# Four attention tiles in float32 instead of nine: where the exponentials and values become float16 pairs

## The chip, the cores and the metric

One core of one Trainium2 chip runs the whole program in one launch. The metric is the device time of one execution in microseconds. The kernel before took 1939.94 us (median of three runs, 1937.46 to 1942.82).

## The reference

Three stages follow one another on 4 sequences of 576 tokens with 8 heads of 64, so 2304 tokens of 512 features:

```
scores = q @ k.T / sqrt(64) - slope[head] * |i - j|     # only for 0 <= i - j < 128
attn   = exp(scores - max) / (sum + 1e-9);  x = attn @ v
x = relu(x @ w_in)**2 @ w_out                            # 512 -> 2048 -> 512
P = exp(x @ w_gate - max), then 8 times: rows / sum, columns / sum, times N/E
out = sum over 8 experts e of P[:, e] * (relu(x @ w1[e]) @ w2[e])   # 512 -> 1024 -> 512
```

q, k and v are float32; w_in and w_out come as float64 words and are narrowed to float32 in the kernel.

## The kernel before

**Pairs.** Most products are computed on float16 pairs: a number is scaled by a power of two and split into a high float16 part (a ScalarE copy) and a low one (the rest, by VectorE or by GpSimd in `minus`, L407). A product of two pairs is three matmuls (high x high, high x low, low x high).

**Attention tiles.** 18 tiles of 128 queries: tiles 0 to 3 and 4 to 7 are the full tiles of sequences 0 and 1, tile 8 holds the 64 last queries of both; 9 to 17 are the same for sequences 2 and 3. A tile needs its own keys and those of the tile before it (`prevs`): tile 0, 4, 9 and 13 have no tile before them, tile 8 needs tiles 3 and 7. Per tile SyncE loads q, k and v into the ring `raw` (8 slots), TensorE turns q and k in float32 (`turn`), and then four steps j of two heads each follow: `scores` (float32 matmuls into one bank), `bias` (VectorE adds the distance and takes the maximum, into a buffer `e`, of which there are 3), `expo` (ScalarE).

From there tiles differ. With `PAIRED = 9` tiles 0 to 8 stay in float32: TensorE turns the exponentials (`turn_e`, L632), ScalarE copies them out of the bank (`turned_e`, L637), and TensorE gathers them with the raw values (`gather`, L654). v's slot of `raw` is held until the next tile has gathered. Tiles 9 to 17 are paired: ScalarE and GpSimd split the exponentials (`e_hi` L520, `e_lo`), SyncE turns both halves by a DMA transpose (`flip_e`, L410), and TensorE gathers pairs (`gather_pairs`, L550). Their values are scaled by a norm (`v_norm` on ScalarE, `v_sum` on TensorE, `v_scale` as small VectorE operations) and split (`v_hi` L499, `v_lo` L502); `join_v` (L515) brings the earlier tile's values to the same scale. The paired values lie in a room of four slots with the tag `yacc`, which is also the tag of block 0's accumulator, so `v_hi` waits for block 0's end (`ready_y[0]`).

Then both kinds divide by the sum, are split and turned by another transpose into xT (`settle`, `x_hi`, `x_lo`, `flip_x`).

**First feed-forward stage.** Blocks hold 4, 2, 4, 4 and 4 tiles, in parts m of 256 tokens (part 0 has 512). For each of 16 slices f of the hidden width: `h_part` (L1032, 12 matmuls of 256 columns), `h_relu` (ScalarE, from the bank to `r`), `h_square` (VectorE, in `r`), `h_hi` and `h_lo`, `y_part` (L1069, 12 matmuls). h has two banks, r two and sq four buffers. Part 0 goes through the four chunks g of w_in and w_out as they come: each chunk is read through SyncE into `stage`, narrowed by VectorE (`narrow`, L887 to L895), scaled and split. The second stage (experts, from about 550 us to the end) is not touched.

**Order.** All of it is planned while the program is built: each step is a unit with an engine, a cost, a rank, the units it waits for and the slots it takes. `Plan.run` plays these costs through and fixes every engine's order; ready units go by rank, and the attention tiles' ranks (100 a tile) stand before those of the feed-forward matmuls. DMAs are all issued by SyncE, in the order of the plan; a waiting one holds up those behind it. Until a planned 66 us `keep_warm` fills TensorE with idle matmuls (L291). The slots of `raw`, `e`, `eT`, `vo` and some more are handed out in the order in which the units were made.

Of the kernel before, what the change touches and what calls it, by code (L numbers as in the profile page):

```python
# [15 lines left out]
HI, LO = 0, 1  # L16
# [131 lines left out]
def kernel(  # L148
# [74 lines left out]
    unit_s = const.tile([P, 2, NCH], F32, name="unit_s")  # L223
# [90 lines left out]
    def make_tail():  # L314
# [10 lines left out]
            raw=8, qT=2, kT=5, s=1, sp=1, diag=1, e=3, eh=2, eT=3, vo=4, vp=1, av=1, x=1, xh=1, x0=1, x1=1, xb=1, yacc=1,  # L325
# [50 lines left out]
    EXPS, TURNED = 3, 3  # L376
# [88 lines left out]
    PAIRED = 9  # L465
    assert not any(x < PAIRED for i in range(PAIRED, NTILE) for x in prevs(i))

# [10 lines left out]
    def v_scale(i):  # L478

        m = main[i]  # L480
        sc = scale_v[i] = small.tile([P, 2], F32, tag="sc", bufs=8, name=f"sc{i}")
        yield from pow2_of_norm((sc[:, 0:1],), m.pop("vss"), 1, WHOLE)
        for x in m["pv"]:
# [5 lines left out]
        for x in m["pv"]:  # L489
            yield  # L490
            f = tiny(1, "fs", bufs=6)
            DVE.tensor_tensor(out=f, in0=scale_v[x][:, 0:1], in1=sc[:, 1:2], op=ALU.mult)
            m["fs"].append(f)

    def v_hi(i):
        if "room" not in values:
            values["room"] = ap_.tile([P, 4, 2, H, D], F16, tag="yacc", name="values")
        values[i] = values["room"][:, plan.got["vo"]]
        ACT.activation(out=values[i][:, HI], in_=raw[i, 2], func=ACTF.Copy, scale=scale_v[i][:, 1:2])  # L499

    def v_lo(i):
        DVE.scalar_tensor_tensor(  # L502
            out=values[i][:, LO], in0=raw.pop((i, 2)), scalar=scale_v[i][:, 1:2], in1=values[i][:, HI], op0=ALU.mult,
            op1=ALU.subtract,
        )
# [156 lines left out]
    def plan_tile(i):  # L662
# [19 lines left out]
        a["kT"], a["v"] = T[1], ld[2]  # L682
        jv = None
        if paired(i):
            n = len(pv)
            u = unit(ACT, c_act(W), v_norm, i, rank=z, after=[ld[2], st])
            mx = unit(PE, 0.3, v_sum, i, rank=z, take=["s"], after=[constants["ones"], u])
            us = chain(DVE, [TINY] * (3 + 2 * n), v_scale, i, rank=z, after=[mx, *(done[p]["sc"] for p in pv)])
# [6 lines left out]
            if pv:  # L695
                older = [] if full else [x for p in pv for x in done[p]["uses"]]
                jv = unit(
                    DVE, 0.43 * n, join_v, i, rank=z + 6, take=["vp"] if full else [],
                    after=[*(done[p]["v"] for p in pv), a["sc"], *older],
                )  # L700
# [29 lines left out]
        for p in (*pv, i):  # L730
            plan.free(done[p]["kT"][0], "kT", *S)
            if not paired(i):
                plan.free(done[p]["v"], "raw", *G)
# [124 lines left out]
    def w_out_scale(g):  # L858

        yield from pow2_of_norm((out_s[:, 0, g : g + 1], out_s[:, 1, g : g + 1]), wst.pop(("out", g)), 1, WHOLE)  # L860
        yield
        DVE.scalar_tensor_tensor(
            out=unit_s[:, 0, g : g + 1], in0=in_s[:, 0, g : g + 1], scalar=in_s[:, 0, g : g + 1],
            in1=out_s[:, 0, g : g + 1], op0=ALU.mult, op1=ALU.mult,
        )
        if g == NCH - 1:
            yield
            m = tiny(2, "cm")
            DVE.tensor_reduce(out=m[:, 0:1], in_=unit_s[:, 0, :], op=ALU.max, axis=AX.X)
# [4 lines left out]
            yield  # L874
            DVE.tensor_scalar(out=gain, in0=m[:, 0:1], scalar1=2.0**14, scalar2=None, op0=ALU.mult)
# [54 lines left out]
    def plan_weights(kind, g, z):  # L930
# [32 lines left out]
        if kind == "out":  # L963
            sq = [unit(ACT, c_act(n), w_sumsq, g, x, rank=z, after=[nr[x], *early]) for x in parts]
            plan.order(sq[1], sq[0])
            ad = unit(DVE, TINY, w_out_add, g, rank=z, after=sq)
            al = unit(PE, 0.3, w_sum, kind, g, rank=z, take=["s"], after=[ad, constants["ones"]])
            us = chain(
                DVE, [TINY] * (8 if g == NCH - 1 else 4), w_out_scale, g, rank=z,
                after=[al, wready["in", g][0], *wready.get(("out", g - 1), [])[:1]],  # L970
            )
            plan.free(al, "s", us[0])
            sc = us[-1]
# [63 lines left out]
    def h_relu(m, f, c):  # L1037
        if f % 2 == 0:
            hold["r", c] = big.tile([P, 2, MC], F32, tag="r", bufs=2, name=f"r{m}_{f}_{c}")
        r = hold["r", f, c] = hold["r", c][:, f % 2]  # L1040
        ACT.activation(out=r, in_=hold.pop(("h", f, c)), func=ACTF.Relu, scale=2.0**-7)  # L1041

    def h_square(m, f, c):
        r = hold["r", f, c]
        g = f // FPC
        if m:
            DVE.scalar_tensor_tensor(out=r, in0=r, scalar=unit_s[:, 1, g : g + 1], in1=r, op0=ALU.mult, op1=ALU.mult)  # L1047
        else:
            DVE.tensor_tensor(out=r, in0=r, in1=r, op=ALU.mult)

    def h_hi(m, f, c):
        if f % 2 == 0:
            hold["sq", c] = big.tile([P, 2, 2, MC], F16, tag="sq", bufs=4, name=f"sq{m}_{f}_{c}")
        sq = hold["sq", f, c] = hold["sq", c][:, f % 2]
        ACT.activation(out=sq[:, HI], in_=hold["r", f, c], func=ACTF.Copy)  # L1055

    def h_lo(m, f, c):
        sq = hold["sq", f, c]
        minus(sq[:, LO], hold.pop(("r", f, c)), sq[:, HI])

    def y_part(m, f, d, c):

        sq = hold["sq", f, c] if d < KD - 1 else hold.pop(("sq", f, c))
        w = pair_of("out", f // FPC)
        first, last = (f % FPC == 0, f % FPC == FPC - 1) if m == 0 else (f == 0, f == KF - 1)
        if first and d % 2 == 0:
            hold["y", d // 2] = pa_.tile([P, 2, MC], F32, tag="ya", bufs=2, name=f"y{m}_{f}_{c}_{d}")
        for a, b in PAIRS:
            PE.matmul(  # L1069
                hold["y", d // 2][:, d % 2], lhsT=w[:, a, f % FPC, d * P : (d + 1) * P], rhs=sq[:, b],  # L1070
# [4 lines left out]
    def y_add(g, c, b):  # L1075
# [3 lines left out]
        y, t, s = hold["yacc"][:, 2 * b : 2 * b + 2, c : c + MC], hold.pop(("y", b)), unit_s[:, 0, g : g + 1]  # L1079
# [8 lines left out]
    def y_src(m, b):  # L1088
        return hold["yacc"][:, b : b + 1] if m == 0 else hold["y", b]
# [6 lines left out]
    def y_max(m, b):  # L1096
        n = y_srcs(m)
        if b == 0:
            hold["ym"] = tiny(n, f"ym{n}")
        DVE.tensor_reduce(  # L1100
            out=hold["ym"][:, b : b + 1], in_=y_src(m, b), op=ALU.max, axis=AX.XY, apply_absolute_value=True
        )
        if b == n - 1:
            t = tiny(1, "ymx")
            DVE.tensor_reduce(out=t, in_=hold["ym"], op=ALU.max, axis=AX.X)
            hold["ym"] = t

# [21 lines left out]
    def y_hi(m, b):  # L1129
# [16 lines left out]
    def plan_block(m):  # L1146
# [10 lines left out]
        for f, c in steps:  # L1157
# [3 lines left out]
            deps = [*xs[(c - c0) // P : (c - c0 + MC) // P], *wready["in", g]]  # L1161
            h0 = unit(PE, c_pe(6, MC), h_part, m, f, c, 0, rank=z - 100 * LEAD, take=["h"], after=deps)
# [207 lines left out]
    free_forms += [lambda: big.tile([P, 2, KH, 2 * P], F16, tag="sq", bufs=4, name="form")] * 4  # L1370
    free_forms += [lambda: big.tile([P, 2, KH, 2 * P], F16, tag="r", bufs=2, name="form")] * 2
# [529 lines left out]
    with tc.manual_schedule():  # L1901
# [11 lines left out]
        for i in range(PAIRED):  # L1913
# [53 lines left out]
```

## Time and profile before

| | us |
|---|---|
| median of three runs | 1939.94 |
| the profiled execution | 1941.23 |
| its span | 1939.5 |
| TensorE busy | 1893.8 (98%) |
| VectorE busy | 1605.7 (83%) |
| ScalarE busy | 1256.2 (65%) |
| GpSimd busy | 938.6 (48%) |

The span runs from the first instruction to the last. Busy time is the union of an engine's instructions. PE is TensorE, PEld its weight loads, DVE VectorE, ACT ScalarE, POOL GpSimd, SP SyncE (SPq: what its queue issues).

### The profile page before, as it was taken

What the parts mean: (1) busy time and instruction counts of PE and PEld (TensorE: products, weight loads), DVE (VectorE), ACT (ScalarE), POOL (GpSimd) and SP (SyncE); (2) the same over time, 40 slices, a digit from 0 to 9 for tenths busy, and PEclk for the clock granted to TensorE, in tenths of its full rate; (3) what the DMA queues carried; (4) which work ended last, traced back from release to release, by engine and by line L of the source; (5) the groups of instructions that cost most, each with busy time, mean ns of one, the idle gap of its engine ahead of it and who ended that gap; (6) DMA issues with size and microseconds to landing.
All of it is one profiled execution on the core that took longest, in us unless ns stands there. A gap on an engine that the chain in (4) does not pass through costs nothing.

```text
span 1939.5 us, 47163 instructions
## 1 busy us (share of the span) xinstructions
PE 1893.8 (98%) x18458; PEld 1680.8 (87%) x18458; DVE 1605.7 (83%) x3897; ACT 1256.2 (65%) x3434; POOL 938.6 (48%) x1198
## 2 busy tenths in 40 slices
PE   9999999999998999999999999999999999999999
PEld 9788888888876888898888989888898888888898
DVE  6796675455549898899989899899989989999887
ACT  5777576354345787666767676676766667666663
POOL 3445354356635654545535445454544545445432
PEclk9999999999999999999999999999999999999999
DMA  9455264210010010110101011000101101010002
GB/s 244 122 145 108 60 117 77 43 52 1 2 45 12 23 34 23 34 33 13 34 23 34 12 34 34 23 23 23 34 13 34 34 23 34 13 34 13 2 23 77
DMA packets 159663, 85.36 MB, mean 44 GB/s; under 512 B 112080, under 2 KB 144848, under 8 KB 159440
## 3 DMA queue, kind: packets, MB, share of 16 engines
q1 hardware_dynamic: 159440, 82.35, 16.6%
q8 instruction: 144, 2.36, 0.5%
q14 instruction: 79, 0.65, 0.1%
HBM read 64.50 MB, written 4.72 MB: 36 GB/s over the span
## 4 chain that ended last, share of the span: by engine, by line
PE 82%; DVE 11%; ACT 3%; DMA 2%; issue 1%; POOL 0%; SPq 0%; DVEq 0%; POOLq 0%; ACTq 0%
PE oX L1520 17%; PE X L1438 16%; PE h L1032 9%; PE oY L1520 8%; PE y L1069 8%; PE Y L1438 8%; PE Z L1438 4%; PE oZ L1520 4%; DVE hp L1501 4%; PE s L593 2%; DVE late L1340 1%; DMA stage<-in_moe_w_dram 1%; PE av L654 1%; PE warm L291 1%; PE t L569 1%
## 5 line engine op out<-in xcount | busy, mean ns | idle before, releaser
L1438 PEld LDWEIGHTS <-late 128*128 128x128 f16 x6720 | 617.8, 98 | 95.1 <-issue 29.6
L1520 PEld LDWEIGHTS <-hp 128*128 128x128 f16 x6048 | 584.0, 98 | 69.4 <-DVE hp L1501 3.3
L1520 PE MATMUL oX<-late,hp 128*128 128x256 f16 x3456 | 468.3, 273 | 2.9 <-DVE hp L1501 2.3
L1501 DVE TENSOR_TENSOR hp<-late,hp 128x256 f16<-128x256 f32 (+1 forms) x669 | 337.4, 524 | 10.1 <-ACT hp L1497 8.1
L1497 ACT ACTIVATE hp<-late 128x256 f16<-128x256 f32 (+1 forms) x669 | 248.0, 387 | 21.3 <-POOL late L1487 7.7
L1501 DVE TENSOR_TENSOR hp<-x,hp 128x256 f16<-128x256 f32 (+1 forms) x451 | 242.9, 549 | 14.7 <-ACT hp L1497 13.3
L1438 PE MATMUL Y<-y,late 128*128 128x256 f16 (+1 forms) x1920 | 241.4, 262 | 1.3 <-ACT late L1466 1.2
L1520 PE MATMUL oY<-late,hp 128*128 128x256 f16 x1728 | 233.5, 273 | 0.0
L1478 ACT ACTIVATE late<-late 128x256 f32<-128x256 f32 (+1 forms) x286 | 111.2, 393 | 165.9 <-DVE late L1470 164.7
L1069 PE MATMUL y<-sq,w_out 128*128 128x256 f16 x1728 | 215.7, 273 | 2.2 <-DVE yacc L1083 1.2
L1438 PE MATMUL X<-late 128*128 128x256 f16 (+1 forms) x1728 | 204.9, 255 | 12.8 <-DVE late L1470 7.4
L1032 PE MATMUL h<-xT,w_in 128*128 128x256 f16 x1728 | 216.4, 274 | 0.0
L407 POOL TENSOR_TENSOR sq<-r,sq 128x256 f16<-128x256 f32 x144 | 106.7, 742 | 211.4 <-ACT sq L1055 204.3
L1069 PEld LDWEIGHTS <-w_out 128*128 128x128 f16 x1728 | 166.4, 98 | 23.5 <-issue 1.7
L1032 PEld LDWEIGHTS <-w_in 128*128 128x128 f16 x1728 | 167.7, 98 | 21.2 <-issue 0.5
L407 POOL TENSOR_TENSOR stage<-stage 128x256 f32<-128x256 f32 x210 | 168.5, 803 | 34.4 <-ACT hp L1497 21.9
L1497 ACT ACTIVATE hp<-x 128x256 f16<-128x256 f32 (+1 forms) x451 | 172.2, 388 | 15.8 <-POOL x L1487 6.2
L1438 PE MATMUL X<-form,late 128*128 128x256 f16 x1152 | 157.1, 272 | 3.7 <-DVE x L1470 2.1
L1340 DVE SCALAR_TENSOR_TENSOR late<-stage,es,late 128x512 f16<-128x512 f32 (+2 forms) x180 | 158.5, 909 | 0.7 <-ACT late L1336 0.6
L1047 DVE SCALAR_TENSOR_TENSOR r<-r,unit_s 128x256 f32<-128x256 f32 x112 | 68.7, 616 | 100.7 <-ACT r L1041 99.9
L1478 ACT ACTIVATE x<-x 128x256 f32<-128x256 f32 (+1 forms) x194 | 74.5, 389 | 118.0 <-DVE x L1470 117.3
L1487 POOL TENSOR_TENSOR late<-late 128x256 f32<-128x256 f32 (+1 forms) x58 | 45.7, 787 | 196.1 <-DVE hp L1501 170.1
(230 smaller groups left out, 3230.9 us busy)
## 6 DMA issues: line engine op xcount, KB each, us to landing
stage<-in_moe_w_dram SPq DMA_DIRECT2D x60, 256.0 KB, 3.2
stage<-in_moe_w_dram SPq DMA_DIRECT2D x30, 512.0 KB, 3.7
st_in<-in_moe_w_in_dram SPq DMA_DIRECT2D x16, 512.0 KB, 6.6
st_out<-in_moe_w_out_dram SPq DMA_DIRECT2D x16, 512.0 KB, 4.8
raw_q<-in_q_dram SPq DMA_DIRECT2D x16, 256.0 KB, 4.4
raw_k<-in_k_dram SPq DMA_DIRECT2D x16, 256.0 KB, 4.3
raw_v<-in_v_dram SPq DMA_DIRECT2D x16, 256.0 KB, 4.5
out_dram<-acc_wc SPq DMA_DIRECT2D x8, 256.0 KB, 2.3
```

Source lines behind the costliest of these rows:

```text
L407: POOL.tensor_tensor(out=dst, in0=src, in1=hi, op=ALU.subtract)
L593: PE.matmul(sp[:, n, P : 2 * P], lhsT=q_, rhs=keys[i][r, j], start=True, stop=True)
L1032: PE.matmul(hp, lhsT=w[:, a, kk, r], rhs=xT[parts1[m][0]][:, b, kk, c : c + MC], start=(kk == 0 and a == b), stop=(kk == KD - 1 and a == LO),)
L1047: DVE.scalar_tensor_tensor(out=r, in0=r, scalar=unit_s[:, 1, g : g + 1], in1=r, op0=ALU.mult, op1=ALU.mult)
L1069: PE.matmul(hold["y", d // 2][:, d % 2], lhsT=w[:, a, f % FPC, d * P : (d + 1) * P], rhs=sq[:, b], start=(first and d % 2 == 0 and a == b) ...
L1340: DVE.scalar_tensor_tensor(out=lo, in0=t, scalar=es[:, g, 2 * kind + 1 : 2 * kind + 2], in1=hi, op0=ALU.mult, op1=ALU.subtract)
L1438: PE.matmul(pt, lhsT=w[:, a, row(kk), :], rhs=rhs, start=(x in (1, 2, 5) and kk == 0 and a == c), stop=(x in (2, 3, 4) and kk == KH - 1 an ...
L1478: ACT.activation(out=t, in_=src, func=ACTF.Relu)
L1487: POOL.tensor_tensor(out=c, in0=c, in1=b, op=ALU.add)
L1497: ACT.activation(out=f[:, HI], in_=hold["t", PLACE[name], g, j, p], func=ACTF.Copy)
L1501: DVE.tensor_tensor(out=f[:, LO], in0=hold["t", PLACE[name], g, j, p], in1=f[:, HI], op=ALU.subtract)
L1520: PE.matmul(pt[:, t], lhsT=f[:, a, t * P : (t + 1) * P], rhs=w[:, c, row], start=(x in (1, 2, 5) and p == t == 0 and a == c), stop=(x in ( ...
```

## The change

`PAIRED` goes from 9 to 4: tiles 4 to 8 are paired too. Tile 3 stays in float32, but since tile 8 needs its values, they are scaled and split as well. The values get a room of five slots of their own, so `v_hi` no longer waits for block 0; `raw` has 6 slots for 8 and `e` 2 for 3. All tiles are planned ahead of all blocks, in one loop each. Small sums on TensorE (`v_sum`, `w_sum` of w_out) wait themselves for what the VectorE chain behind them needed. From part 2 on `h_square` multiplies h, still in its bank, by relu(h) in `r`, with the factor 2^-7 in a third column of `unit_s`; the bank is freed by the square, and h waits for w_out's last scale. The names kept in `hold` carry the part, and r and sq take fixed slots.

```diff
-    unit_s = const.tile([P, 2, NCH], F32, name="unit_s")
+    unit_s = const.tile([P, 3, NCH], F32, name="unit_s")
-            raw=8, ..., e=3, eh=2, eT=3, vo=4, ...
+            raw=6, ..., e=2, eh=2, eT=3, vo=5, ...
-    EXPS, TURNED = 3, 3
+    EXPS, TURNED = 2, 3
-    PAIRED = 9
+    PAIRED, VALUES = 4, 5
 def v_scale(i):
+        pv = m["pv"] if paired(i) else []
 def v_hi(i):
-            values["room"] = ap_.tile([P, 4, 2, H, D], F16, tag="yacc", name="values")
+            values["room"] = ap_.tile([P, VALUES, 2, H, D], F16, tag="values", name="values")
 def plan_tile(i):
-        if paired(i):
-            n = len(pv)
+        if paired(i) or any(i in prevs(x) for x in range(PAIRED, NTILE)):
+            n = len(pv) if paired(i) else 0
-            mx = unit(PE, 0.3, v_sum, i, rank=z, take=["s"], after=[constants["ones"], u])
-            us = chain(DVE, ..., v_scale, i, rank=z, after=[mx, *(done[p]["sc"] for p in pv)])
+            mx = unit(PE, 0.3, v_sum, ..., after=[constants["ones"], u, *(done[p]["sc"] for p in pv if n)])
+            us = chain(DVE, ..., v_scale, i, rank=z, after=[mx])
-            vh = unit(ACT, c_act(W), v_hi, i, rank=z + 9, take=["vo"], after=[a["sc"], *ready_y[0]])
+            vh = unit(ACT, c_act(W), v_hi, i, rank=z + 9, take=["vo"], after=[a["sc"]])
-            a["v"] = unit(DVE, c_dve(W, 1.17), v_lo, i, rank=z + 11, after=[vh])
-            plan.free(ld[2], "raw", a["v"])
+            a["vl"] = unit(DVE, c_dve(W, 1.17), v_lo, i, rank=z + 11, after=[vh])
+            plan.free(ld[2], "raw", a["vl"])
+            if paired(i):
+                a["v"] = a["vl"]
 def w_out_scale(g):
+            DVE.tensor_scalar(out=unit_s[:, 2, :], in0=unit_s[:, 1, :], scalar1=2.0**-7, ...)
 def plan_weights(kind, g, z):
-            al = unit(PE, 0.3, w_sum, kind, g, rank=z, take=["s"], after=[ad, constants["ones"]])
+            al = unit(PE, 0.3, w_sum, ..., after=[ad, constants["ones"], wready["in", g][0], ...])
 def h_square(m, f, c):
-            DVE.scalar_tensor_tensor(out=r, in0=r, scalar=unit_s[:, 1, g : g + 1], in1=r, ...)
+            s = unit_s[:, 1 + (m > 1), g : g + 1]
+            DVE.scalar_tensor_tensor(out=r, in0=h if m > 1 else r, scalar=s, in1=r, ...)
 def plan_block(m):
+            if m > 1:
+                deps.append(wready["out", NCH - 1][0])
-            plan.free(h0, "h", r)
+            q_.shared = m < 2
+            plan.free(h0, "h", q_ if m > 1 else r)
 ...
-        for i in range(PAIRED):
+        for i in range(NTILE):
             plan_tile(i)
-        plan_block(0)
-        for i in range(PAIRED, NTILE):
-            plan_tile(i)
-        for m in range(1, NM):
+        for m in range(NM):
             plan_block(m)
```

## Rows read from the trace of the kernel before

**Rows 1.** Busy time of each engine by stretch; bracketed are instruction counts.

```profile
core 0: us, PE busy (x) PEld busy (x) DVE busy (x) ACT busy (x) POOL busy (x), PEclk, DMA share, GB/s
66.00:84.00 18.00, 15.05 (x133) 13.40 (x134) 13.78 (x47) 14.33 (x37) 7.39 (x5) 1.00 0.15 31
84.00:140.00 56.00, 53.56 (x479) 46.49 (x479) 47.59 (x112) 42.23 (x96) 30.29 (x29) 0.97 0.60 161
140.00:183.00 43.00, 43.00 (x395) 36.27 (x396) 30.16 (x87) 32.64 (x80) 19.21 (x19) 1.00 0.34 88
183.00:236.00 53.00, 53.00 (x495) 45.85 (x493) 30.82 (x103) 32.59 (x94) 19.99 (x26) 1.00 0.40 72
236.00:400.00 164.00, 161.44 (x1786) 137.47 (x1783) 101.32 (x308) 96.84 (x281) 70.67 (x81) 1.00 0.45 81
400.00:550.00 150.00, 148.21 (x1412) 131.80 (x1410) 73.54 (x132) 62.78 (x146) 90.55 (x106) 1.00 0.04 14
```

**Rows 2.** The filler tile: ns min/median/max, then first and last start, forms.

```profile
L291 PE MATMUL warm<-ones x460: 219/219/314, 1.1 to 65.8; 128*128 128x128 f16 x154
```

**Rows 3.** The gathers' tile, as above.

```profile
L654 PE MATMUL av<-raw_v,eT x272: 222/275/323, 14.0 to 181.3; 128*128 128x64 f32 x120, 128*64 128x64 f32 x16
L550 PE MATMUL av<-values,eT x264: 189/193/217, 235.8 to 389.6; 128*128 128x64 f16 x108, 128*64 128x64 f16 x24
```

**Rows 4.** SyncE's queue in order of time: start, us, what is issued.

```profile
79.34 1.23 SPq L410 DMA_TRANSPOSE xT<-xh  x1
...
104.64 1.27 SPq L389 DMA_DIRECT2D raw_k<-in_k_dram  x2
122.28 1.27 SPq L389 DMA_DIRECT2D raw_v<-in_v_dram  x2
123.73 3.27 SPq L813 DMA_DIRECT2D st_in<-in_moe_w_in_dram  x4
```

**Rows 5.** Groups on TensorE, 0 to 700 us: busy us, mean ns; then idle before.

```profile
L1032 PE MATMUL h<-xT,w_in 128*128 128x256 f16 x1728 | 216.4, 274 | 0.0
...
L654 PE MATMUL av<-raw_v,eT 128*128 128x64 f32 x240 | 32.4, 271 | 0.0
...
L632 PE MATMUL et<-ident,e 128*128 128x128 f32 x128 | 20.4, 277 | 0.5 <-ACT eT L637 0.5
...
L550 PE MATMUL av<-values,eT 128*128 128x64 f16 x216 | 14.7, 193 | 0.4 <-DVE x L420 0.4
...
L265 PE MATMUL total<-vss,ones 128*128 128x1 f32 x18 | 3.2, 249 | 0.0
L654 PE MATMUL av<-raw_v,eT 128*64 128x64 f32 x32 | 2.7, 246 | 0.0
...
L550 PE MATMUL av<-values,eT 128*64 128x64 f16 x48 | 2.3, 203 | 0.0
```

**Rows 6.** Groups on ScalarE, 0 to 550 us.

```profile
L1041 ACT ACTIVATE r<-h 128x256 f32<-128x256 f32 x142 | 53.9, 380 | 91.7 <-PE h L1032 91.2
...
L520 ACT ACTIVATE eh<-e 128x512 f16<-128x512 f32 x28 | 17.0, 617 | 0.0
L637 ACT ACTIVATE eT<-et 128x512 f32<-128x512 f32 x28 | 16.6, 594 | 15.3 <-PE et L632 15.2
```

**Rows 7.** Groups on GpSimd, 0 to 550 us.

```profile
L407 POOL TENSOR_TENSOR eh<-e,eh 128x512 f16<-128x512 f32 x28 | 33.7, 1210 | 20.2 <-ACT eh L520 10.4 <-issue 3.8 <-PE av L550 3.3
```

**Rows 8.** Groups on VectorE, 0 to 550 us.

```profile
L502 DVE SCALAR_TENSOR_TENSOR values<-raw_v,sc,values 128x512 f16<-128x512 f32 x9 | 7.7, 874 | 0.4 <-ACT values L499 0.3
```

**Rows 9.** The turned exponentials' tile: ns min/median/max.

```profile
L410 SPq DMA_TRANSPOSE eT<-eh x36: 1188/1233/1361, 189.0 to 383.5; - x36
```

**Rows 10.** Three lines on VectorE: ns min/median/max.

```profile
L1047 DVE SCALAR_TENSOR_TENSOR r<-r,unit_s x112: 465/485/1490, 210.5 to 553.3; 128x256 f32<-128x256 f32 x112
...
L1470 DVE TENSOR_TENSOR late<-X,late x12: 275/411/426, 605.3 to 793.4; 128x256 f32<-128x256 f32 x10, 128x128 f32<-128x128 f32 x2
...
L891 DVE SCALAR_TENSOR_TENSOR bits_out<-st_out,bits_out x8: 1214/1225/2183, 34.0 to 164.5; 128x1024 int32<-128x1024 int32 x8
```

More of the change, by code (lines that the diff above doesn't have):

```diff
@@ L488, in v_scale @@
         m["fs"] = []
-        for x in m["pv"]:
+        for x in pv:
             yield
@@ L502, in v_lo @@
         DVE.scalar_tensor_tensor(
-            out=values[i][:, LO], in0=raw.pop((i, 2)), scalar=scale_v[i][:, 1:2], in1=values[i][:, HI], op0=ALU.mult,
+            out=values[i][:, LO], in0=raw[i, 2], scalar=scale_v[i][:, 1:2], in1=values[i][:, HI], op0=ALU.mult,
             op1=ALU.subtract,
@@ L698, in plan_tile @@
                     DVE, 0.43 * n, join_v, i, rank=z + 6, take=["vp"] if full else [],
-                    after=[*(done[p]["v"] for p in pv), a["sc"], *older],
+                    after=[*(done[p]["vl"] for p in pv), a["sc"], *older],
                 )
@@ L732, in plan_tile @@
             if not paired(i):
-                plan.free(done[p]["v"], "raw", *G)
+                plan.free(ld[2] if p == i else done[p]["ld"], "raw", *G)
             elif full and p != i:
@@ L874, in w_out_scale @@
             yield
+            DVE.tensor_scalar(out=unit_s[:, 2, :], in0=unit_s[:, 1, :], scalar1=2.0**-7, scalar2=None, op0=ALU.mult)
+            yield
             DVE.tensor_scalar(out=gain, in0=m[:, 0:1], scalar1=2.0**14, scalar2=None, op0=ALU.mult)
@@ L966, in plan_weights @@
             ad = unit(DVE, TINY, w_out_add, g, rank=z, after=sq)
-            al = unit(PE, 0.3, w_sum, kind, g, rank=z, take=["s"], after=[ad, constants["ones"]])
-            us = chain(
-                DVE, [TINY] * (8 if g == NCH - 1 else 4), w_out_scale, g, rank=z,
-                after=[al, wready["in", g][0], *wready.get(("out", g - 1), [])[:1]],
+            al = unit(
+                PE, 0.3, w_sum, kind, g, rank=z, take=["s"],
+                after=[ad, constants["ones"], wready["in", g][0], *wready.get(("out", g - 1), [])[:1]],
             )
+            us = chain(DVE, [TINY] * (9 if g == NCH - 1 else 4), w_out_scale, g, rank=z, after=[al])
             plan.free(al, "s", us[0])
@@ L1025, in h_part @@
         if x == 0:
-            hold["h", f, c] = ps.tile([P, MC], F32, tag="h", bufs=2, name=f"h{m}_{f}_{c}")
-        hp = hold["h", f, c]
+            hold["h", m, f, c] = ps.tile([P, MC], F32, tag="h", bufs=2, name=f"h{m}_{f}_{c}")
+        hp = hold["h", m, f, c]
         w = pair_of("in", f // FPC)
@@ L1038, in h_relu @@
         if f % 2 == 0:
-            hold["r", c] = big.tile([P, 2, MC], F32, tag="r", bufs=2, name=f"r{m}_{f}_{c}")
-        r = hold["r", f, c] = hold["r", c][:, f % 2]
-        ACT.activation(out=r, in_=hold.pop(("h", f, c)), func=ACTF.Relu, scale=2.0**-7)
+            hold["r pair", m, c, f // 2] = big.tile([P, 2, MC], F32, tag=f"r{plan.got['r']}", name=f"r{m}_{f}_{c}")
+        r = hold["r", m, f, c] = hold["r pair", m, c, f // 2][:, f % 2]
+        ACT.activation(out=r, in_=hold["h", m, f, c], func=ACTF.Relu, scale=2.0**-7)
     def h_square(m, f, c):
-        r = hold["r", f, c]
+        r, h = hold["r", m, f, c], hold.pop(("h", m, f, c))
         g = f // FPC
         if m:
-            DVE.scalar_tensor_tensor(out=r, in0=r, scalar=unit_s[:, 1, g : g + 1], in1=r, op0=ALU.mult, op1=ALU.mult)
+            s = unit_s[:, 1 + (m > 1), g : g + 1]
+            DVE.scalar_tensor_tensor(out=r, in0=h if m > 1 else r, scalar=s, in1=r, op0=ALU.mult, op1=ALU.mult)
         else:
@@ L1052, in h_hi @@
         if f % 2 == 0:
-            hold["sq", c] = big.tile([P, 2, 2, MC], F16, tag="sq", bufs=4, name=f"sq{m}_{f}_{c}")
-        sq = hold["sq", f, c] = hold["sq", c][:, f % 2]
-        ACT.activation(out=sq[:, HI], in_=hold["r", f, c], func=ACTF.Copy)
+            hold["sq pair", m, c, f // 2] = big.tile([P, 2, 2, MC], F16, tag=f"sq{plan.got['sq']}", name=f"sq{m}_{f}_{c}")
+        sq = hold["sq", m, f, c] = hold["sq pair", m, c, f // 2][:, f % 2]
+        ACT.activation(out=sq[:, HI], in_=hold["r", m, f, c], func=ACTF.Copy)
     def h_lo(m, f, c):
-        sq = hold["sq", f, c]
-        minus(sq[:, LO], hold.pop(("r", f, c)), sq[:, HI])
+        sq = hold["sq", m, f, c]
+        minus(sq[:, LO], hold.pop(("r", m, f, c)), sq[:, HI])
     def y_part(m, f, d, c):
-        sq = hold["sq", f, c] if d < KD - 1 else hold.pop(("sq", f, c))
+        sq = hold["sq", m, f, c] if d < KD - 1 else hold.pop(("sq", m, f, c))
         w = pair_of("out", f // FPC)
@@ L1088, in y_src @@
     def y_src(m, b):
-        return hold["yacc"][:, b : b + 1] if m == 0 else hold["y", b]
+        return hold["yacc"][:, b : b + 1] if m == 0 else hold["y", m, b]
     def y_dst(m, a, b):
@@ L1098, in y_max @@
         if b == 0:
-            hold["ym"] = tiny(n, f"ym{n}")
+            hold["ym", m] = tiny(n, f"ym{n}")
         DVE.tensor_reduce(
-            out=hold["ym"][:, b : b + 1], in_=y_src(m, b), op=ALU.max, axis=AX.XY, apply_absolute_value=True
+            out=hold["ym", m][:, b : b + 1], in_=y_src(m, b), op=ALU.max, axis=AX.XY, apply_absolute_value=True
         )
@@ L1369 @@
     free_forms = [lambda n=n: form_at(n) for n in range(7)]
-    free_forms += [lambda: big.tile([P, 2, KH, 2 * P], F16, tag="sq", bufs=4, name="form")] * 4
-    free_forms += [lambda: big.tile([P, 2, KH, 2 * P], F16, tag="r", bufs=2, name="form")] * 2
+    free_forms += [
+        lambda tag=tag: big.tile([P, 2, KH, 2 * P], F16, tag=tag, name="form")
+        for tag in ("sq0", "sq1", "sq2", "sq3", "r0", "r1")
+    ]
     def quarter(j, a, r, c):
```

36 lines of the change are left out of this document (19 added, 17 removed).

## The prediction

> **What bounds the kernel now.** I read the page's first two parts first: TensorE is busy in 98% of the span, and one of the 40 slices alone shows it under 0.9. A busy share says little alone, because part of it is filler, so the second view is the table of stretches [rows 1]. From 84 us to 550 us, the end of the first feed-forward stage, TensorE stands idle for 2.44 + 0 + 0 + 2.56 + 1.79 = 6.8 us of 466 us; VectorE, ScalarE and GpSimd all have more room than that. Third view, one tile: the filler matmuls that keep the engine warm end at 65.8 us [rows 2]. So what TensorE does after 66 us is work, and each microsecond taken out of it is taken out of the time, provided other work is ready in its place. Before 66 us that does not hold: there the filler takes up whatever TensorE is spared.
>
> The tiles in float32 gather from 14.0 to 181.3 us, the tiles in pairs from 235.8 us on [rows 3]: a paired tile's first pass on its values waits for block 0 to end, since values and block 0's accumulator share one room. Tile 3, the last one of block 0, has its output turned at 79.34 us [rows 4], so tiles 4 to 8, which change form, lie almost wholly after 66 us, in the stretch where TensorE bounds.
>
> **What the change removes and adds on TensorE.** Durations are shares of busy time per record [rows 5]; a float32 product shows as two records, a pair product as three.
> Removed for tiles 4 to 8: gathers, 8 + 3 x 16 + 8 = 64 products of full width, 128 records at 32.4/240 = 0.135 us, 17.3 us; the tail tile's half products, all 32 records, 2.7 us; the turns of the exponentials, 8 + 3 x 16 + 16 = 72 at 20.4/128 = 0.159 us, 11.5 us. Together 31.5 us.
> Added: 64 x 3 = 192 pair products at 14.7/216 = 0.068 us, 13.1 us; half products as in tile 17, 2.3 us; the sum of squares of the values for tiles 3 to 8, 6 x 2 records at 3.2/18 = 0.178 us, 2.1 us. Together 17.5 us.
> Net on TensorE: -14.0 us. All of it counts, by the first part, if idle time does not grow.
>
> **Beside TensorE, tiles 3 to 8.** ScalarE: the copy of turned exponentials (0.594 us) is replaced by the copy to the high half (0.617 us) [rows 6], which is even; two passes over the values come in, about 0.62 us each by the same rows, 6 x 2 x 0.62 = 7.4 us. GpSimd: the low halves, 16 at 1.21 us and 4 at half width, an estimate of 22 us [rows 7]. VectorE: a low half of the values at 0.874 us for six tiles [rows 8], four joins of about that size and some 6 small operations each, an estimate of 14 us. Between 84 and 236 us these engines have 45, 83 and 43 us free (ScalarE, GpSimd, VectorE, from the same table) [rows 1]. So I cost them at nothing; if that cover is gone, weights come later, which is a rival below. SyncE: 20 more transposes at 1.23 us of issue [rows 9], 25 us, in a queue that also carries the weights' reads; it has the room, but it is in order, and a transpose waits at its head for GpSimd's low half with everything behind it. That too is a rival.
>
> **Values in their own room.** The wait for block 0's end goes from tiles 9 to 17: they can start after 181 us instead of 236 us. That itself saves nothing, because TensorE was busy in that stretch with block 0 (183 to 236 us: no idle) [rows 1]; it only swaps the order of the work. What it can save is idle time later on: at most 2.56 + 1.79 = 4.35 us. What is late next is the raw ring: it shrinks from 8 to 6 and the exponentials' buffers from 3 to 2. In the trace a load of v stands at SyncE's head from 105.91 us (104.64 + 1.27) to 122.28 us, 16.4 us, with the four reads of the last chunk of w_in behind it [rows 4]. With six slots such stands can get longer or come earlier; paired tiles give v back earlier, after two passes instead of after the next tile's gather, so from tile 4 on they get shorter. I take nothing, and keep one stand as the upper end.
>
> **The squares.** From block 2 on a square reads h from its bank and r from SBUF. The trace does not show this form. Nearest: the square now, 485 ns median, and an addition of a bank and a tile of the same size, 411 ns [rows 10]. 96 squares give between -7 us and, were a bank 0.1 us dearer, +10 us of VectorE, which has over half its time free after 236 us; I take -7 us, and nothing for the time. The bank is held longer, until the square. Twelve records of h take 12 x 216.4/1728 = 1.5 us [rows 5], y the same; with two banks and h and y in turn the bank is wanted 3 x 1.5 = 4.5 us after its h ends, and relu (0.38 us, [rows 6]) plus square (0.49 us) plus handing over need some 1.5 us. Cover gone means h back to back, a bank wanted after 1.5 us: a few tenths each for the first 6 of six parts, at most 36 x 0.2 = 7 us; at least nothing. I take nothing, since these runs stand beside y and attention of other parts.
>
> **Moved waits.** The sums for values and w_out now wait on TensorE's side for all that the small VectorE chain needs, so the one small bank is not held by a sum whose reader waits. Behind the waiting matmul stands TensorE's own order. The planner places it when its inputs are due; a miss costs TensorE directly, one wait of 0 to 3 us for 5 tiles. I put +2 us for this and for the new order's other misses, and the gain from the freed bank at nothing. The names by part and the fixed tags of r and sq add no instruction. The wait of h from part 2 on for w_out's last scale is met long before.
>
> **Sum.** -14.0 + 2 = -12.0 us. The profiled execution took 1941.23 us with a span of 1939.5 us, 1.7 us around it, and would take 1929.2 us; the median shown is 1939.94 us, 1.3 us less than the profiled one, and becomes 1927.9 us. I say 1928. The likeliest case's own range is 1923 to 1932. A run of this kernel can be told from no change from about 0.3%, 5.8 us, on: under 1934.1 or over 1945.8 us.
>
> **Rivals.**
> More than the sum: the 4.35 us of idle after 236 us go, since attention ends early and parts find their tiles ready; no misses come in. -18.4 us, 1921.6 us. For it: those waits are late ones, of attention's end. Against: idle in a fixed order comes back elsewhere.
> Weights come late through VectorE. From 84 to 140 us it is busy 47.59 of 56 us [rows 1], and TensorE already loses 2.44 us there. Values of tiles 3 to 6 want some 9 us in it. And the narrowing of weights slows beside GpSimd: 1.225 us median, 2.183 us at most [rows 10]. Eight such passes for chunk 2, each 0.96 us late, are 7.7 us of idle: -14.0 + 7.7 = -6.3, 1933.6 us; with the full stretch, 10 us, 1936. The Trainium skill, page "SBUF — State Buffer", section "Who interferes with whom", says that a VectorE instruction with two SBUF inputs is shut out for as long as a GpSimd instruction that reads SBUF holds the port that both use. By that rule each pass could lose a whole low half of 1.21 us, 8 x 1.21 = 9.7 us, and the sum would be -4.3, 1935.6 us. The trace's longest passes agree with it, its medians show that it is seldom met.
> The tiles are no quicker: what bounds tiles 4 to 8 is their chain through one score bank, and TensorE waits out its 14 us from 84 to 236 us for lack of weights and tiles. 1940. Against: no idle at all there from 140 us on [rows 1].
> The start slips (the slower side). Place: SyncE's queue ahead of tile 3's transpose at 79.34 us [rows 4]; block 0's second half needs that tile, and TensorE has nothing else then (2.95 us idle between 66 and 84 us already) [rows 1]. With six raw slots a load can stand there as the one at 122.28 us did. One stand: -12 + 16.4 = +4.4, 1944; both slots that are lost, -12 + 32.8 = +20.8, 1961. It decides from a stand of 12 us on. For it: the float32 tiles hold v through the next tile's gather. Against: tiles 0 to 3 have 80 us for 12 loads.
>
> **Chances.** Forecast 0.46; more than the sum 0.12; weights late 0.17, of it 0.07 under 1934; no quicker 0.08; start slips 0.17, of it 0.13 over 1946. Faster by over 0.3%: 0.46 + 0.12 + 0.07 = 0.65. Within: 0.10 + 0.08 + 0.04 = 0.22. Slower: 0.13. The range 1919 to 1944 reaches below the best case by 2.6 us, what pair products dearer or cheaper by a fifth would make (13.1/5), and above to one stand; it leaves out the rest of the last rival, 0.13, and little below.
>
> **What would show it.** Right: the turns of exponentials fall from 128 to 56 records and the float32 gathers to 112 and none of half width; the pair products of float16 rise to 552 and 96; TensorE's busy time falls by about 14 us; block 0's h after tile 3 still starts by 84 to 87 us; paired gathers begin by 110 us; idle from 84 to 550 us stays under 10 us, and the stage ends near 538 us with the rest as long as before. Wrong: the stage ends early but the later one is longer; tile 3's transpose comes past 90 us; or idle between 84 and 183 us above 12 us, with the waits on weights or on SyncE.

## The result: slower by 0.6%

The changed kernel takes 1953.28 us (median of three runs, 1951.57 to 1954.13) for 1939.94 us, a ratio of 1.0057 with a 95% interval of 1.0041 to 1.0073. Forecast were 1928 us and a range of 1919 to 1944. TensorE did get its work taken off, and lost more than that to idle time and to its lower clock, nearly all of it between 66 and 190 us.

The stretches of the changed kernel, with the columns of [rows 1]:

```profile
66.00:84.00 18.00, 16.39 (x115) 14.09 (x115) 13.37 (x41) 12.10 (x23) 6.23 (x6) 0.81 0.26 57
84.00:140.00 56.00, 44.12 (x400) 35.94 (x399) 49.68 (x104) 38.09 (x94) 34.50 (x33) 0.94 0.69 166
140.00:183.00 43.00, 33.46 (x303) 27.22 (x301) 31.33 (x73) 26.51 (x62) 23.11 (x23) 0.80 0.47 118
183.00:236.00 53.00, 50.97 (x528) 42.01 (x526) 38.93 (x113) 34.20 (x94) 28.98 (x30) 1.00 0.49 93
236.00:400.00 164.00, 163.42 (x1802) 138.56 (x1801) 100.41 (x336) 107.23 (x318) 73.53 (x84) 1.00 0.54 91
400.00:550.00 150.00, 149.12 (x1462) 133.43 (x1460) 67.47 (x153) 65.90 (x152) 87.17 (x106) 1.00 0.07 18
```

Between 84 and 183 us TensorE is idle for 11.9 + 9.5 us where [rows 1] had 2.4 + 0. Its granted clock is 0.81, 0.94 and 0.80 of full speed in the first three stretches, a mean of full and half speed; before, one of them had 0.97.

Now each kernel in one line: from 66 us to the last record of y, which ends the first stage (568.9 us before, 578.9 us after). The kernel before, then the changed one:

```profile
66.00:568.90 502.90, 491.00 (x4832) 425.83 (x4833) 301.96 (x802) 290.32 (x752) 239.96 (x266) 1.00 0.32 69
```

```profile
66.00:578.90 512.90, 484.74 (x4846) 415.44 (x4847) 308.07 (x838) 296.22 (x769) 258.25 (x287) 0.97 0.38 78
```

Idle rises from 11.9 to 28.2 us, +16.3; busy time falls by 6.3 us only, because part of the work ran at the lower clock. The sum is +10.0 us, and the second stage is as long as before (1370.6 and 1370.9 us), so nearly the whole loss of the profiled execution (+10.3 us of span) is here.

Where the work went, in groups of TensorE as in [rows 5]:

```profile
L550 PE MATMUL av<-values,eT 128*128 128x64 f16 x336 | 23.6, 193 | 0.0
L654 PE MATMUL av<-raw_v,eT 128*128 128x64 f32 x112 | 16.8, 297 | 0.4 <-ACT eT L637 0.4
L632 PE MATMUL et<-ident,e 128*128 128x128 f32 x56 | 9.5, 289 | 1.8 <-ACT qT L578 1.0 <-ACT eT L637 0.7
L265 PE MATMUL total<-vss,ones 128*128 128x1 f32 x30 | 4.9, 231 | 0.4 <-ACT kT L578 0.2
```

The counts are as worked out; the float32 groups are dearer per record (297 ns mean for 271), which is the clock.

What it waited for, longest first (us in total, times, longest), from 84 to 190 us, TensorE and then VectorE:

```profile
PE s L593 <- DVE nmax L607: 8.6, 1, 8.6
PE total L265 <- DVE wom L855: 4.3, 2, 3.0
PE h L1039 <- POOL w_in L407: 2.2, 2, 1.7
```

```profile
DVE e L607 <- POOL eh L407: 6.7, 2, 4.8
```

The longest one, 8.6 us up to 165.25 us, is a score matmul at the head of TensorE's queue: it waits for a bias, that waits for one of the two buffers e, and that for GpSimd's low half, which stood behind two low halves of the weights and, before them, low halves of squares for which GpSimd waited on ScalarE three times. VectorE is busy for only 4.3 of the 10 us from 156 to 166 us, so a full VectorE is not what this wait stands on (columns as in [rows 1]):

```profile
156.00:166.00 10.00, 1.40 (x12) 1.12 (x12) 4.29 (x10) 5.89 (x13) 8.20 (x9) 0.77 0.28 95
```

The weights come later. The last low halves of w_out start at 201.9 us in the changed kernel, at 183.0 us in the kernel before:

```profile
L407 POOL TENSOR_TENSOR w_out<-st_out,w_out x16: 1145/1165/2146, 61.4 to 201.9; 128x512 f16<-128x512 f32 x16
```

```profile
L407 POOL TENSOR_TENSOR w_out<-st_out,w_out x16: 1148/1162/2139, 58.6 to 183.0; 128x512 f16<-128x512 f32 x16
```

The attention tiles come later still. Each tile's output is turned by one transpose; tile 4's and tile 7's, in the kernel before:

```profile
100.96 1.24 SPq L410 DMA_TRANSPOSE xT<-xh  x1
...
173.49 1.74 SPq L410 DMA_TRANSPOSE xT<-xh  x1
```

In the changed kernel, tile 3's, which is still in float32, then tile 4's and tile 7's:

```profile
86.41 1.24 SPq L410 DMA_TRANSPOSE xT<-xh  x1
...
136.10 1.24 SPq L410 DMA_TRANSPOSE xT<-xh  x1
...
238.21 1.24 SPq L410 DMA_TRANSPOSE xT<-xh  x1
```

One cause of the late weights is a thing that the prediction never looked at. There is one slot (`diag`) for the diagonal of a maximum; the chunks of w_in and the gate's small weights (`mx`) both use it, and the sum over it needs the one small bank `s`. In VectorE's and TensorE's order of the changed kernel, the gate's diagonal is written at 83.70 us, its sum runs at 116.35, and only then comes chunk 2's:

```profile
83.70 1.08 DVE L270 TENSOR_SCALAR diag<-ident,mx 128x128 f32<-128x128 f32 x1
...
116.35 0.49 PE L265 MATMUL total<-diag,ones 128*128 128x128 f32 x2 [0.40 <-DVE pn L238]
...
119.01 0.96 DVE L270 TENSOR_SCALAR diag<-ident,wmm 128x128 f32<-128x128 f32 x1
```

Both halves of chunk 2's maximum were there by about 100.5 us. The kernel before has the same hold, from 77.65 to 105.61 us, with chunk 2's maximum there at about 97 us and its diagonal at 107.27 us. So the hold itself is 32.7 us for 28.0, and chunk 2 waits 18.5 us for 10.4.

### The profile page after: what moved, and what is told of

Its sections match the earlier page's. It is cut to its first block, busy times and chain, and to the rows that moved or that the text cites. A ratio compares the mean times of both kernels' runs of the same rounds, so it can differ in the third digit from the quotient of the medians.

```text
span 1949.8 us, 47345 instructions
## 1 busy us (share of the span) xinstructions
PE 1888.0 (97%) x18478; PEld 1670.5 (86%) x18478; DVE 1612.8 (83%) x3937; ACT 1263.5 (65%) x3452; POOL 955.6 (49%) x1218
## 4 chain that ended last, share of the span: by engine, by line
PE 76%; DVE 15%; ACT 3%; DMA 3%; issue 2%; POOL 1%; SPq 0%; DVEq 0%; POOLq 0%; ACTq 0%
PE oX L1534 16%; PE X L1452 16%; PE oY L1534 8%; PE y L1078 8%; PE Y L1452 8%; PE h L1039 7%; DVE hp L1515 4%; PE Z L1452 4%; PE oZ L1534 4%; DMA stage<-in_moe_w_dram 2%; PE s L593 1%; DVE late L1352 1%; PE av L550 1%; DVE late L1484 1%; DVE acc_wc L1560 1%
## 5 line engine op out<-in xcount | busy, mean ns | idle before, releaser
L1348 ACT ACTIVATE late<-stage,es 128x512 f16<-128x512 f32 (+2 forms) x180 | 135.1, 783 | 3.8 <-DVE es L246 3.8
```

Of the source, the lines that this page charges most:

```text
L1348: ACT.activation(out=hi, in_=t, func=ACTF.Copy, scale=es[:, g, 2 * kind + 1 : 2 * kind + 2])
```

## The experiments

Times are medians beside runs of the kernel before on the same chip, whose median was 1940.4 to 1942.1 us. "Idle" is TensorE's from 66 us to the first stage's end.

**p9: all of the change but the pairing.**

```diff
-    PAIRED, VALUES = 4, 5
+    PAIRED, VALUES = 9, 5
```

> Theories: A, the pairing of tiles 4 to 8 takes 14 us off TensorE, but VectorE and GpSimd get its work in the stretch from 84 to 190 us in which they also narrow and split the weights, so weights and tiles come late, TensorE idles and falls to its lower clock. B, the smaller buffers (raw 6, e 2) hold up the fixed order. C, squares that read h from its bank hold the h banks too long. This run keeps every other edit and has PAIRED = 9 again. A: the loss goes, 1934 to 1943 us, idle of TensorE from 84 to 190 us under 6 us. B: the loss stays, 1948 to 1955. C: the loss stays too.

1992.85 us, ratio 1.0268 (1.0253 to 1.0283). None of A, B and C had this: without pairing the rest of the change costs 51 us. The trace shows where; the gate's diagonal and chunk 2's on VectorE, 76.7 and 184.6 us:

```profile
L270 DVE TENSOR_SCALAR diag<-ident,wmm x2: 281/285/289, 184.6 to 211.7; 128x128 f32<-128x128 f32 x2
L270 DVE TENSOR_SCALAR diag<-ident,mx x1: 289/289/289, 76.7 to 76.7; 128x128 f32<-128x128 f32 x1
```

The gate held the slot for 105 us, with tiles 4 to 8 in float32 and its first sum over values at 159.6 us. That gave theory D, below.

**nobank: the squares put back.**

```diff
-            DVE.scalar_tensor_tensor(out=r, in0=h if m > 1 else r, scalar=s, in1=r, ...)
+            DVE.scalar_tensor_tensor(out=r, in0=r, scalar=unit_s[:, 1, g : g + 1], in1=r, ...)
-            plan.free(h0, "h", q_ if m > 1 else r)
+            plan.free(h0, "h", r)
```

> Only the squares are put back: r times r from part 2 on, the bank freed by relu. A and B: within 4 us of the changed kernel, 1949 to 1957 us, with the 8.6 us of idle near 157 us still there. C: 1940 us or less.

1954.5 us, as the changed kernel, and the wait of 8.6 us is still there: C is out.

**wfirst: weights ranked before tiles 4 to 8.**

```diff
-            z["in", g], z["out", g] = 300 + 100 * g, 310 + 100 * g
+            z["in", g], z["out", g] = 300 + 10 * g, 305 + 10 * g
```

> Only the ranks of the weights change: chunks 1 to 3 rank 310 to 335 and so stand before tiles 4 to 8 wherever both are ready. A: the last weights come by 180 us or earlier for 202 us, idle from 84 to 190 us falls from 21 us to under 10, 1930 to 1941 us. B: the small buffers hold tiles as before, 1946 us or more. C: 1950 to 1957.

1950.7 us. The weights came earlier (w_out's last low half at 168.4 us), and idle rose to 31.1 us for 28.2. A's time and its idle are missed (12.9 us from 84 to 190 us, where it wanted under 10); the time lies in the ranges of B and of C, so this run takes nothing from B.

**e3v4: three buffers for e, four values.**

```diff
-            ... e=2, eh=2, eT=3, vo=5, ...
+            ... e=3, eh=2, eT=3, vo=4, ...
-    EXPS, TURNED = 2, 3
+    EXPS, TURNED = 3, 3
```

> Three buffers for e again, paid for by a room of four values for five (tile 3 holds one of them until tile 8, three go round). raw stays at 6. B: most of the loss goes, 1938 to 1945 us, no wait of bias on GpSimd's low halves over 1 us. A: within 4 us of the changed kernel, 1949 to 1957 us.

1946.48 us, ratio 1.0022 (1.0013 to 1.0032): between A and B, 6.8 us under the changed kernel. B's sign is missed: in this run too a bias waits 3.9 us for a low half, and the longest wait of a score matmul is 8.9 us.

**gl_after, gl_p9, gl_before, gl_e3v4: the gate's chain behind the weights.** The one edit, made in the changed kernel, in p9, in the kernel before and in e3v4:

```diff
-        u = unit(DVE, 0.1, gate_max, rank=7000, after=[u])
+        u = unit(DVE, 0.1, gate_max, rank=7000,
+                 after=[u, *wready["in", NCH - 1][:1], *wready["out", NCH - 1][:1]])
```

> Theory D: one slot for the diagonal of a maximum serves the weights and the gate's weights alike. In the changed kernel the gate's chain takes it at 83.7 us and its sum waits for the one small bank until 116.4 us, so chunk 2's diagonal comes at 119.0 us for 107.3 us before; the new sums over values and more tiles in flight crowd that bank. Here only the gate's chain waits for the last weights' scales. D: chunk 2's diagonal by 105 us, its weights ready by 120 us for 132, 1935 to 1946 us. A (VectorE and GpSimd are full with the pairs' work) and B (small buffers): idle stays, only moved, 1948 to 1957 us.

1940.46 us, ratio 0.9992 (0.9983 to 1.0001): 12.8 us under the changed kernel. Chunk 2's diagonal comes at 101.0 us, w_out's last low half at 185.4 us. Chunk 2's last low half of w_in ends at 128 us, which is earlier than in the changed kernel but not by 120 us.

> PAIRED = 9 and the rest of the change gave 1993 us: there the gate held the slot from 76.7 to 181.8 us. With the gate's chain behind the weights, D: 40 us or more come back, 1938 to 1955 us. What stays over 1942 us is the price of the smaller buffers and the new order for float32 tiles (B). If it stays over 1980 us, D is wrong and B alone is at work.

1939.37 us, 0.9990 (0.9981 to 1.0000): 53 us come back, all that p9 had lost, and chunk 2's diagonal is at 91.6 us. So with tiles 4 to 8 in float32 the smaller buffers and the new order cost nothing that can be seen once the slot is free, and B falls there.

> The same edit in the kernel before, where the gate held the slot from 77.7 to 105.6 us and chunk 2's maximum was ready by 97 us. D: TensorE's 2.4 us of idle between 84 and 140 us go, and not more can, since it has none until 340 us: 1936 to 1942 us. If D counts for more than idle time, it would be under 1934.

1938.75 us, 0.9984 (0.9975 to 0.9994): as expected, and the lowest median of a kernel that does all the work, though 0.6 us under gl_p9 is within the intervals.

> The gate's chain behind the weights and three buffers for e (with four values), in the changed kernel. D and B together, if they add: the 7 us that e gave and what the gate gives, 1928 to 1940 us. A alone: 1944 us or more.

1942.44 us, 1.0007 (0.9997 to 1.0017), between the two ranges. The two do not add: with the gate out of the way, the third buffer for e gives nothing, so B falls for the paired tiles too.

So freeing the slot takes the loss of 13 us away, and the question is turned round: gl_after and gl_p9 differ by the pairing alone, which should be worth 14 us, and take the same time. gl_after, then gl_p9, to the first stage's end:

```profile
66.00:567.60 501.60, 480.92 (x4851) 411.91 (x4849) 308.21 (x838) 298.50 (x771) 262.08 (x287) 0.99 0.38 80
```

```profile
66.00:566.10 500.10, 489.78 (x4855) 424.89 (x4853) 293.48 (x799) 291.19 (x753) 235.22 (x267) 1.00 0.33 71
```

Busy time is 8.9 us less, idle is 20.7 us for 10.3. The clock of gl_after by stretch:

```profile
66.00:84.00 18.00, 16.31 (x117) 13.81 (x114) 13.21 (x39) 11.94 (x24) 6.07 (x5) 0.81 0.23 50
84.00:140.00 56.00, 49.13 (x450) 40.37 (x450) 49.71 (x111) 44.22 (x103) 36.93 (x35) 0.97 0.75 186
140.00:183.00 43.00, 36.48 (x365) 30.96 (x363) 37.78 (x82) 29.98 (x69) 31.33 (x29) 0.96 0.42 102
```

0.19 x 18 + 0.03 x 56 + 0.04 x 43 = 6.8 us of full speed are missing, against none in gl_p9. The work at full clock is then between 8.9 and 15.7 us less, which holds the 14.0 of the forecast.

**cut_after and cut_p9: VectorE relieved of two chunks' narrowing**, both with the gate's chain behind the weights.

```diff
 def narrow(kind, g, x, step):
+        if g >= 2:
+            if step == 2:
+                stage[kind, g, x] = top.bitcast(F32)
+            return
```

> Leaves out the narrowing of chunks 2 and 3 of w_in and w_out (24 passes of VectorE, some 27 us, between 96 and 190 us; their values are then not the weights'), in the changed kernel with the gate's chain behind the weights. To be read against cut_p9. A (the pairs' work on VectorE and GpSimd meets the weights' there): with VectorE relieved TensorE's saving comes through, this is 8 to 14 us under cut_p9. If the saving on TensorE is not real or is lost elsewhere (low clock for other reasons, buffers): within 4 us of cut_p9.

> The same left out with PAIRED = 9. TensorE has 3.8 us of idle from 66 to 236 us in the uncut one, so all theories: 1934 to 1940 us, at most 5 us under it.

1927.45 and 1932.83 us (four runs each, 1925.7 to 1929.0 and 1930.6 to 1935.6). The pairs now gain 5.4 us where they had lost 1.1; idle is 13.2 us for 4.9. That lies between the two expectations: A has a part of its size. cut_p9 gained 6.5 us over gl_p9 where at most 5 were expected, so leaving the narrowing out gains time without the pairs too. Both kernels were planned anew with the narrowing at no cost, so their orders differ as well.

**cut2_after and cut2_p9: GpSimd relieved too.**

```diff
 def w_lo(kind, g, x, y):
+        if g >= 2:
+            POOL.memset(w[:, LO, c].bitcast(F32), 0.0)
+            return
```

> Beside the narrowing of chunks 2 and 3 this leaves out their low halves too: GpSimd sets them to zero, 16 operations of some 0.3 us for 1.3 us. If GpSimd, which also splits the exponentials of tiles 4 to 8, holds up what is left, idle of TensorE from 66 to 236 us falls under 6 us and this comes 9 to 14 us under cut2_p9. If not, the difference stays where it was between cut_after and cut_p9, 5.4 us, give or take 3.

> The same left out with PAIRED = 9. TensorE had 1.9 us of idle from 66 to 236 us with the narrowing cut alone, so nothing is to be gained: 1929 to 1935 us by either theory.

1927.75 and 1934.47 us: 6.7 us of gain, not 9 to 14, and no difference from 5.4 that the runs could tell. TensorE's idle time from 66 to 236 us is 9.0 us in cut2_after, not under 6. cut2_after, then cut2_p9:

```profile
66.00:555.00 489.00, 476.31 (x4852) 409.85 (x4850) 279.80 (x814) 296.87 (x771) 239.41 (x287) 0.99 0.39 82
```

```profile
66.00:563.20 497.20, 489.07 (x4854) 426.12 (x4852) 264.04 (x773) 290.98 (x753) 216.69 (x267) 1.00 0.33 71
```

Here TensorE's saving is seen best: 12.8 us less busy, idle 12.7 us for 8.1. By these two runs GpSimd's share of the weights was not what held the rest.

**gl_p6: tiles 4 and 5 in float32.**

```diff
-    PAIRED, VALUES = 4, 5
+    PAIRED, VALUES = 6, 5
```

> The gate's chain behind the weights, and PAIRED = 6: tiles 4 and 5, which stand among the weights of chunks 1 and 2, stay in float32, tiles 6 to 8 are paired. TensorE saves some 10 us instead of 14. A: their pairs' work falls partly behind the last weights, idle from 66 to 236 us is nearer to the 3.8 us of PAIRED = 9 than to the 16.6 us of PAIRED = 4: 1930 to 1937 us. B or lost elsewhere: 1938 to 1944.

1940.28 us, 1.0001 (0.9991 to 1.0010), idle 18.0 us, 15.2 of it from 66 to 236 us: a miss for A. Moving the pairs two tiles on does not free the stretch.

**gl_wfirst: both the gate's chain and the weights' ranks.**

> The gate's chain behind the weights and the weights' ranks before tiles 4 to 8, in the changed kernel. A: with the weights first on the crowded engines the last of them come by 170 us for 185, 1930 to 1938 us. If the tiles then come too late for block 1, TensorE idles near 190 us instead and it stays at 1938 to 1946.

1956.16 us: outside both ranges and worse than either alone, idle 33.1 us.

**gl_warm and gl_before_warm: a longer filler.**

```diff
-    WARM, COLD, IDLE = 230, 24, 66.0
+    WARM, COLD, IDLE = 420, 24, 110.0
```

> The changed kernel with the gate's chain behind the weights, and filler matmuls wherever the plan has TensorE idle until a planned 110 us instead of 66 (up to 420 pairs for 230). In gl_after TensorE ran at its lower clock from 69.8 to 76.7 and from 86.9 to 90.3 us. If that costs time of the end: 1934 to 1939 us and clock 1.00 from 66 to 140 us. If TensorE waited for weights and tiles there anyway: within 2 us of 1940.5.

> The kernel before with the gate's chain behind the weights and the same longer filler. It lost 3 us to idle from 66 to 84 us and ran 3.4 us at the lower clock after it. If the clock counts: 1934 to 1938 us; if not, 1938 to 1940 as without the filler.

1953.42 and 1943.71 us. Both miss their ranges. The clock stayed at 1.00 from 66 to 84 us, and the time rose by 13 and 5 us. The likely reason is that the filler stands in TensorE's fixed order before real work that came earlier than planned: in gl_warm 9.1 us of it run after 66 us, for 0.3 in gl_after. No run shows that by itself. What the clock alone costs is not settled by it.

**gl_cost and gl_cost_r7: a plan with costs nearer to the measured ones**, the second with more buffers.

```diff
-    TINY = 0.08
+    TINY = 0.15
-                f, cost = gather_pairs, 0.17 * nk
+                f, cost = gather_pairs, 0.41 * nk
...
-            raw=6, ..., e=2, eh=2, eT=3, vo=5, ...      # gl_cost_r7 only
+            raw=7, ..., e=3, eh=2, eT=3, vo=3, ...
```

> The changed kernel with the gate's chain behind the weights, planned with costs nearer to the measured ones: small VectorE steps 0.15 for 0.08, pair gathers 0.41 a block for 0.17, scores 0.1 + 0.37 for 0.1 + 0.22 a block, bias 1.1 for 0.78, exponentials 1.38 for 0.97, joins 0.9 for 0.43, float32 gathers 0.54 for 0.45. If the remaining idle is a fixed order that was planned too tight, 1930 to 1937 us. If VectorE and GpSimd are simply full there, 1938 to 1943 us whatever the order.

> The same with 7 slots of raw, 3 buffers of e and 3 values (for 6, 2 and 5). If the small buffers hold up tiles 0 to 3, tile 3 is turned by 80 us for 86 and this is 3 us or more under gl_cost; if not, within 3 us of it.

1955.82 and 1971.53 us, both slower than gl_after and outside what was expected, with idle 32.1 and 32.3 us. Better costs did not give a better order. wfirst, gl_wfirst, gl_warm and gl_cost move no work at all or little, and swing the time by 3 to 16 us: so much hangs on which order comes out. A single order's 13 us, as in gl_after, is therefore shown by the times of its steps (chunk 2 at 101.0 for 119.0 us) and by gl_p9's 53 us, rather than by the total alone. The gains of 5.4 and 6.7 us between the cut kernels have no such second witness.

## Why the prediction was wrong

**"Net on TensorE: -14.0 us"** was right: the counts are exact, and the work is 8.9 to 15.7 us less in gl_after than in gl_p9, and 12.8 us or more less between the cut2 kernels.

**"All of it counts, by the first part, if idle time does not grow"**, with +2 us for all misses, is the step that failed. Idle grew by 16.3 us and the lower clock stretched what work there was. The prediction's own sign of being wrong came true: 21.4 us of idle between 84 and 183 us, where it allowed 12, though the longest wait stands on a bias and not on weights or SyncE. Three terms were missing or too small:

The gate's hold on the slot `diag`, 12.8 us (changed kernel against gl_after). It was in the trace of before, 28 us long; since TensorE had only 2.4 us of idle behind it there, nothing pointed to it in a table of busy time. The hold grew by only 5 us, and the gate ranks behind the tiles and the weights for the small bank in both kernels. But the same edit gained 2.4 us in the kernel before and 12.8 in the changed one. One reading, which the later tiles support and no run shows by itself, is that TensorE had less other work ready in the meantime. What sets the length of the hold is not shown. It is not the pairing of tiles 4 to 8 or the sums over their values, since p9 has neither and held the slot longest. It was none of the rivals.

VectorE in the weights' stretch. **"So I cost them at nothing"** rested on 43 us free between 84 and 236 us. From 96 to 146 us the changed kernel has VectorE busy for 9.8 to 10.0 of every 10 us. The kernel before has 9.8 to 9.9 from 96 to 126 us, with TensorE full beside it, so the load alone settles nothing; the cut kernels are what speaks for it. One such stretch, the kernel before, then the changed one:

```profile
116.00:126.00 10.00, 10.00 (x97) 9.20 (x95) 9.82 (x24) 8.84 (x25) 6.07 (x5) 1.00 0.20 40
```

```profile
116.00:126.00 10.00, 7.47 (x79) 6.09 (x80) 9.78 (x33) 7.10 (x18) 5.46 (x6) 1.00 0.37 74
```

The rival "weights come late through VectorE" had the place, and a price of 8 to 10 us; relieving VectorE gave 6.5 us (from +1.1 to -5.4). Its mechanism, slower passes of the narrowing, was the smaller part: the 16 passes with two inputs between 84 and 190 us took 23.1 us for 21.3, 1.8 us more and not 7.7.

The clock. The sum had no term for it. At 1.2 GHz a stretch counts 0.50 and at 2.4 GHz 1.00, so by the first three stretches 0.19 x 18 + 0.06 x 56 + 0.20 x 43 = 15.4 us of full speed are missing in the changed kernel, and 1.7 us in the kernel before. Part of that is idle time. TensorE fell to the lower level after or while it stood idle (1.6 us between 66 and 70 us, 1.7 us up to 85.9 us, 4 us between 136 and 142 us, and the 8.6 us wait), but not each time: from 116 to 126 us (shown above) it idled 2.5 us and stayed at 1.00. Where work follows at the lower level, an idle stretch costs more than its length. How much in all, no run separates; as an estimate, if the work fell by the forecast's 14.0 us and the busy time by 6.3, the rest, some 8 us, is work at the lower level.

**"The tiles are no quicker"**, with its 1940 us, is where gl_after stands, and the rows above show tiles 4 to 8 not only no quicker but later: tile 7's output is turned at 238.21 us for 173.49, and in gl_after at 226.1 us for 171.8 in gl_p9. The rival put it on the one score bank. A paired tile also goes through GpSimd and a transpose in SyncE's queue before it is gathered, and no run takes one of these alone away, so this rival stands untested beside VectorE.

**"The start slips"**: tile 3's transpose came at 86.41 us for 79.34 [rows 4]. That is 7 us of slip where the rival needed 12, and idle between 66 and 84 us did not rise (1.6 us for 2.95), though the clock there was 0.81 for 1.00. Whether it is a part of the loss, and of what size, no run shows.

**Values' own room** took away the wait as said: pair gathers start at 96.8 us for 235.8 [rows 3]. Idle from 236 to 550 us fell from 4.35 to 1.46 us, 2.9 us of the 4.35 that the first rival hoped for. The prediction took 550 us for the end of the stage, which is at 568.9 us; so its 538 us was 19 us too early from the start, which does not touch the sum.

**The squares** cost nothing in time, as said (nobank). The forecast's -7 us of VectorE came from a shorter operation and did not come that way: they take 484 ns in the median, as before. But none is over 485, where [rows 10] had up to 1490, and the mean up to 550 us fell from 618 to 481 ns, 13 us for 96 squares:

```profile
L1056 DVE SCALAR_TENSOR_TENSOR r<-h,unit_s,r x96: 466/484/485, 271.6 to 564.0; 128x256 f32<-128x256 f32 x96
```

What stays open: why some 7 us of TensorE's 14 do not come through even with both engines relieved (6.7 us gained). The candidates that are left are the order itself, the clock and the tiles' longer way. One more stands in the kernel and was not tested: `Plan.run` starts no step marked `shared` (all of GpSimd's and some of VectorE's, its narrowing, low halves and joins among them) while one of the other engine runs in the plan. So in the plan the pairs' low halves take turns with the narrowing, and the 83 and 43 us that the prediction found free on the two engines could not be counted in full side by side.

## What to carry to other kernels

A saving on the busiest engine is worth its size only where the others can deliver sooner; read the engines' load in the stretch where the work moves, in tens of microseconds, not over a phase. Ask of every slot and bank of which there is one who can hold it longest: a step of the lowest rank that takes a slot early and then waits for a contended bank blocks everyone behind it. What that costs changes with the rest of the plan: freeing one slot was worth 2 us in the kernel before, 13 in the changed one and 53 in p9, and no line of the gate's was touched between them. In a plan with a fixed order, judge an edit by when its steps run and not by the total of one order alone.

## What the hardware showed besides

One of VectorE's smallest operations with two operands in SBUF took 1 us: in the changed kernel `wmm` at 117.92 us, one element a partition, took 0.98 us, for 0.15 us in the kernel before, while GpSimd ran three multiplications on q:

```profile
117.92 0.98 DVE L777 SCALAR_TENSOR_TENSOR wmm<-wmm,mxu 128x1 int32<-128x1 int32 x1
```

```profile
117.84 3.04 POOL L559 TENSOR_TENSOR raw_q<-raw_q,head 128x512 f32<-128x512 f32 x3
```

The Trainium skill, page "SBUF — State Buffer", section "Who interferes with whom", has a VectorE instruction with two SBUF inputs shut out while a GpSimd instruction that reads SBUF holds the shared port, and one with at most one SBUF input, outside the 2-port modes, not. Both sides agree with this trace: this operation waits out most of a GpSimd instruction (its three take 1.0 us each), and the squares that read h from its bank have no slow ones among 96. The two writes of `diag` shown above have one tile as input and took 1.08 and 0.96 us, for 0.27 and 0.29 us in the kernel before; whether they ran in a 2-port mode no run here shows. The forecast's 0.96 us was the right size for one such meeting, and too much for every narrowing pass: 16 passes lost 1.8 us together.
